# Lending two one-bank product tiles as a third score slot in the w_out stages

## The chip, the cores and the metric

The kernel runs on one core of one Trainium2 chip. The metric is device time in microseconds (us), median over several executions. All runs quoted here are of the undisturbed (fast) state; the granted TensorE clock was 0.996 to 1.000 of full speed in all of them, 0.998 to 1.000 in the profiled ones. Ratios are computed from the mean time of one kernel's fast runs over the mean time of the fast runs of the kernel before in the same rounds, so they are not quite the ratio of the quoted medians.

## The reference, cut to what matters

```python
# q, k, v: (8, 12, 448, 64)
scores = matmul(q, k.transpose(0, 1, 3, 2)) / sqrt(64)
attn   = maximum(scores, 0) ** 2 / 448
x      = matmul(attn, v)            # heads joined: (3584, 768)
h      = x @ w_in                   # (768, 2048)
g      = maximum(h, 0) ** 2
out    = g @ w_out                  # (2048, 768)
```

## The kernel before

TensorE is kept busy with the two dense stages, "w_in" (x @ w_in) and "w_out" (g @ w_out), in turn for each pair of batches. The attention of later batches is slipped in between as **visits**. A visit computes the scores of up to two tiles (four 64x64 matmuls each) and, when a head unit's seven tiles are squared, one attention-times-v unit (28 matmuls of 64x64), which I call an "av".

Scores go to one of two slots of two PSUM banks each; ScalarE evicts a slot with one ACTIVATE, and VectorE squares the result.

```python
def score(t, times=1, third=False):
    ...
    ps = slot(FP32, third)                      # two slots, two banks each
    ... nc.tensor.matmul(ps[c, hh, 0:S], ...)
    at = at_p.tile([P, 2, S], FP16, ...)
    nc.scalar.activation(out=at, in_=ps[:, :, 0:S], func=AF.Relu, scale=SK)
```

In w_out a **group** makes two row blocks by a scheme of seven products of eight matmuls each, numbered here 0 to 6 as in the code. They accumulate in two one-bank tiles X and Y; groups take turns between two pairs of such tiles. Product 0 of the next group is placed before product 5 of this one. At the end of a stage a mere six small w_in matmuls stand there.

```python
products = (                # accumulator, fresh, left, right, what follows
    (X, True,  ..., b11, end1),     # 0: copy m1 on ScalarE
    (Y, True,  ..., b21, end2),     # 1: output add on VectorE
    (X, False, ss[2], t2, end6),    # 2: copy u2 on ScalarE, then sum s3 on VectorE
    (Y, True,  ss[1], t1, end5),    # 3: sum s4 on VectorE
    (X, False, ss[3], t3, end7),    # 4: needs s3; copy u3 on ScalarE
    (X, False, ..., nt4, end4),     # 5: writes X again
    (Y, False, ss[4], b22, end3))   # 6: output add on VectorE
```

VectorE's order is planned on the host. The squares of a visit wait in a queue `due`; before a sum, those that the plan calls nearly ready are issued:

```python
def sums(i, rows, to):
    ...
    while due and due[0][0] <= max(at_ve[0], at_pe[0]) + 0.3:
        put(due)                    # a square
    now_ve(0.6)
    op(to[i], x, y)                 # the sum s1, s2, s3 or s4
...
def visit(tiles):                   # cut
    at_pe[0] += 0.19 + 0.19 * len(tiles)
    for i, t in enumerate(tiles):
        square(ats[t], 0.6 + 0.85 * i)
```

Of the kernel before, what the change touches and what calls it, by code (L numbers as in the profile page):

```python
# [12 lines left out]
FP32 = mybir.dt.float32  # L13
AF = mybir.ActivationFunctionType
# [4 lines left out]
def kernel(  # L19
# [9 lines left out]
    nc = tc.nc  # L29

    B, H, S, D = q.shape
    NT, DM = out.shape
# [11 lines left out]
    J = 7  # L44
    PW = S // J
    NU = 3
    NUN = B * NU
# [7 lines left out]
    SK = 256.0  # L55
    CX = 1.0 / 896.0
# [137 lines left out]
    def slot(dtype, third=False):  # L194
        return (third_p if third else s_p).tile(
            [P, 2, 2048 // mybir.dt.size(dtype)], dtype, name="slot", tag="slot")
# [54 lines left out]
    now = [0]  # L251
    avt = [None]

    def score(t, times=1, third=False):
        n, j = divmod(t, J)
        qT, kT = qkt[n]
        ps = slot(FP32, third)
        for hh in list(range(2)) * times:
            r = slice(64 * hh, 64 * hh + 64)
            for hp in range(2):  # L260
                c = slice(64 * hp, 64 * hp + 64)
                nc.tensor.matmul(  # L262
                    ps[c, hh, 0:S], lhsT=kT[r, j, c], rhs=qT[r, :, c],
                    start=True, stop=True)
        at = at_p.tile([P, 2, S], FP16, name="at", tag="at")
        nc.scalar.activation(out=at, in_=ps[:, :, 0:S], func=AF.Relu, scale=SK)  # L266
        ats[t] = at
        seen[t] = now[0]

# [28 lines left out]

    unit = [NU]

    def av_unit():

        n = unit[0]
        if n == NUN or seen.get(n * J + J - 1, 10 ** 6) >= now[0]:
            return
        unit[0] += 1
        flush(rest=False)
        at_pe[0] += 1.33
        b, u = divmod(n, NU)
        vt = vts[n]  # L310
        ps = slot(FP32)
        for j in range(J):
            at = ats.pop(n * J + j)
            for hp in range(2):
                r = slice(64 * hp, 64 * hp + 64)
                for hh in range(2):
                    nc.tensor.matmul(  # L317
                        ps[64 * hh:64 * hh + 64, hp, 0:S],
                        lhsT=vt[r, hh, j * D:(j + 1) * D], rhs=at[r, hh, :],
                        start=(j == 0), stop=(j == J - 1))  # L320
        if u == 0:
            xts[b] = x_p.tile([P, NM, S], FP16, name="xt", tag="xt")
        nc.scalar.activation(
            out=xts[b][:, 2 * u:2 * u + 2, :], in_=ps[:, :, 0:S],
            func=AF.Copy, scale=CX)

    def prefetch(m):
        if m >= NUN:
            return
        dma_transpose(m)  # L330
        if m > NPE:
            load_v(m)
        if m + 2 < NUN:
            load_qk(m + 2)
# [10 lines left out]
    def flush(rest=True):  # L345
        for d in (due, due_g) if rest else (due,):
            while d:
                put(d)

    def put(d):  # L350
        ready, cost, fn, _ = d.popleft()
        at_ve[0] = max(at_ve[0], at_pe[0], ready) + cost
        fn()

    def fill(until):
        for d in (due, due_g):
            while d and max(at_ve[0], at_pe[0], d[0][0]) + d[0][1] <= until:
                put(d)
# [8 lines left out]
    def square(at, lag=0.0):  # L367
        due.append((at_pe[0] + lag, 0.54,
                    lambda: nc.vector.tensor_mul(at, at, at), 0))  # L369

    def visit(tiles):
        now[0] += 1
        for t in tiles:
            if t % J == 0 and t >= NPE * J:
                prefetch(t // J + 2)
        for t in tiles[:1]:
            score(t)
        av_unit()
        for t in tiles[1:]:
            score(t)  # L380
        at_pe[0] += 0.19 + 0.19 * len(tiles)
        for i, t in enumerate(tiles):
            square(ats[t], 0.6 + 0.85 * i)
# [5 lines left out]
    def mm_tile(i=None, dtype=FP32):  # L389
        if i is None:  # L390
            mm_no[0] += 1
            i = mm_no[0] % len(big)
        return big[i].tile(
            [P, 2048 // mybir.dt.size(dtype)], dtype, name="mm", tag="mm")
# [45 lines left out]
    def sums_x(b, i):  # L440
        xt = xts[b]
        lo, hi = slice(0, NH), slice(NH, NM)
        b11, b12, b21, b22 = (xt[:, lo, 0:Q], xt[:, lo, Q:S], xt[:, hi, 0:Q],
                              xt[:, hi, Q:S])
        now_ve(0.42)
        if i != 2:
            t = late["xs"].tile([P, NH, Q], FP16, name=f"x{i}", tag=f"x{i}")
            xsum[b, i] = t
        if i == 0:
            nc.vector.tensor_sub(t, b12, b11)  # L450
        elif i == 1:
            nc.vector.tensor_sub(t, b22, xsum[b, 0])
        elif i == 2:
            nc.vector.tensor_sub(b12, b22, b12)
        else:
            nc.vector.tensor_sub(t, b21, xsum[b, 1])
# [139 lines left out]
    def o_groups(groups, then):  # L596
# [5 lines left out]
        def group(n, rows, last):  # L602
# [7 lines left out]
            def needs(k):  # L610

                return max(2 * p + (tb > 2) for p, tb in groups[k]
                           if (p, tb) not in saved)

            def ahead(i, k=n):
                if k < len(groups) and i not in sets[k]:
                    flush_g(needs(k))
                    sums(i, groups[k], sets[k])
# [95 lines left out]
            def step(k, f):  # L714
                acc, fresh, left, right, end = products[k]
                if last and k == 5:
                    acc, fresh = Z, True

                def run():
                    if f == 0 and fresh and k != 3:  # L720
                        acc[:] = [mm_tile((n + (k == 5)) % 2)]
                    if f == 0 and k == 0:
                        ahead(1)
                        ahead(2)
                    nc.tensor.matmul(  # L725
                        acc[0][:, 0:HALF], lhsT=left()[:, f], rhs=right[:, f],
                        start=(fresh and f == 0),
                        stop=(f == KH - 1), skip_group_check=not fresh)
                    if f == KH - 1:
                        end()  # L730
                        if k < 4 and n + 1 < len(groups):
                            some = sum(d[3] <= needs(n + 1) for d in due_g)
                            for _ in range(-(-some // (4 - k))):
                                put(due_g)
                        fill(at_pe[0] + AFTER[k])
                return run

            ls = [[(0.1625, step(k, f), ((2 if k == 5 else True) if f == 0 else False))
                   for f in range(KH)] for k in range(7)]
            if last:  # L740
                ls[6] = [(0.0825, step3(z, f), False) for z in range(2) for f in range(KH)]
# [34 lines left out]
    NB0 = NU * J  # L776
    ps = slot(FP32, True)
# [3 lines left out]
    def s(t, times=2):  # L781
        score(t, times, third=t in THIRD)
# [81 lines left out]
    def some(part):  # L864
# [11 lines left out]
        name="mmb", bufs=2, space=PSUM, side="right", reuse_waits="tile")))  # L876
    some(f0[4:6])
    visit([NB0, NB0 + 1])

    T_G = NM * 0.1892  # L880
# [5 lines left out]
    events = []  # L886
    seq = [[2, 3], 4, [4, 5], [6, 7], [8, 9], 5, [10, 11], [12, 13], [14, 15],
           [16, 17], [18, 19], [20], []]
    for i, ts in enumerate(seq):
        at = (2.5 + i) * T_G  # L890
        if isinstance(ts, int):
            events.append((at, lambda n=ts: pe_transpose(n)))
        else:
            events.append((at, lambda ts=ts: visit([NB0 + t for t in ts])))
# [14 lines left out]
    for m in (6, 7):  # L909
        events.append((T_H + (1 + 3 * (m - 6)) * T_G, lambda m=m: prefetch(m)))  # L910
    at0 = T_H + 8 * T_G
    for pr in range(1, B // 2):
        t0 = 2 * NB0 * pr
        end = begin[pr] + T_S - 6.5
        gap = (end - at0) / 21
        for i in range(21):
            ts = [t0 + 2 * i, t0 + 2 * i + 1]
            events.append((at0 + i * gap, lambda ts=ts: visit(ts), True))
        at0 = end
        for i in range(4):  # L920
            events.append((begin[pr] - 6 + i, lambda b=2 * pr, i=i: sums_x(b, i)))
    events.append((at0 + 0.3, lambda: visit([]), True))

    def pre(pr, i):
        def run():
# [29 lines left out]
                steps += periods[b, i0]  # L955
        steps += outs[pr][0]

    clock, last = 0.0, 0.0
    ev = deque(sorted(events, key=lambda e: e[0]))
    for cost, fn, edge in steps:  # L960
        fired = 0
        while ev and edge and ev[0][0] <= clock + (1.6 if edge == 2 and not fired else 1e-3):
            if len(ev[0]) == 3:
                if clock < last + 1.5:
                    break
                last = clock
            ev.popleft()[1]()
            fired += 1
        if fn is not None:
            at_pe[0] += cost  # L970
            fn()
        clock += cost
# [31 lines left out]
```

## Time and profile before

| | before |
|---|---|
| median of the first 3 runs (370.80 us with the fourth, run beside the changed kernel) | 370.99 us |
| profiled span | 368.9 us |
| TensorE busy | 359.6 us, 97% |
| VectorE, ScalarE busy | 265.4 us (72%), 247.5 us (67%) |
| visits from 60 us on | 64 |

In a row of the chain of waits the share is that of the span for which the line held up the end. In a timeline row the columns are the start and the length in us, engine, source line, operation, operands, how often, and in brackets the idle time before it with what ended it. Visits are counted as unbroken runs of 64x64 weight loads (PEld) between loads of 128x128.

### The profile page before, as it was taken

What the parts mean: (1) busy time and instruction counts of PE and PEld (TensorE: products, weight loads), DVE (VectorE), ACT (ScalarE), POOL (GpSimd) and SP (SyncE); (2) the same over time, 40 slices, a digit from 0 to 9 for tenths busy, and PEclk for the clock granted to TensorE, in tenths of its full rate; (3) what the DMA queues carried; (4) which work ended last, traced back from release to release, by engine and by line L of the source; (5) the groups of instructions that cost most, each with busy time, mean ns of one, the idle gap of its engine ahead of it and who ended that gap; (6) DMA issues with size and microseconds to landing.
All of it is one profiled execution on the core that took longest, in us unless ns stands there. A gap on an engine that the chain in (4) does not pass through costs nothing.

```text
span 368.9 us, 8720 instructions
## 1 busy us (share of the span) xinstructions
PE 359.6 (97%) x3588; PEld 230.3 (62%) x3588; DVE 265.4 (72%) x470; ACT 247.5 (67%) x371; POOL 107.1 (29%) x128
## 2 busy tenths in 40 slices
PE   8899999999999999999999999999999999999994
PEld 3644445445555778875555588786555689976663
DVE  2997677997777787788585766989766686884442
ACT  3988894787676989876556588886765885532220
POOL 8545521846553155531225045140000000000001
PEclk9999999999999999999999999999999999999999
DMA  8999999999999999967699899692323300003333
GB/s 115 191 207 203 205 204 162 161 158 165 190 166 127 184 101 98 115 93 62 140 166 105 159 155 86 88 116 37 65 71 88 85 3 2 2 0 85 87 92 81
DMA packets 121159, 42.64 MB, mean 116 GB/s; under 512 B 100832, under 2 KB 117760, under 8 KB 121120
## 3 DMA queue, kind: packets, MB, share of 16 engines
q0 software_dynamic: 82912, 23.01, 62.3%
q1 hardware_dynamic: 38048, 18.98, 25.7%
q8 instruction: 28, 0.46, 0.5%
q10 hardware_dynamic: 160, 0.10, 0.1%
q14 instruction: 11, 0.09, 0.1%
HBM read 45.61 MB, written 11.01 MB: 153 GB/s over the span
## 4 chain that ended last, share of the span: by engine, by line
PE 90%; ACT 3%; DVE 3%; issue 2%; DMA 1%; POOL 0%; POOLq 0%; ACTq 0%
PE mm L725 34%; PE mm L538 27%; PE slot L262 10%; PE mm L409 9%; PE slot L317 7%; ACT at L266 3%; DMA k<-in_k_dram 1%; DVE at L297 1%; PE avt L280 1%; PE slot L238 1%; PE mm L238 0%; DVE at L369 0%; DVE xt L292 0%; ACT u L627 0%; DVE osb L632 0%
## 5 line engine op out<-in xcount | busy, mean ns | idle before, releaser
L266 ACT ACTIVATE at<-slot 128x896 f16<-128x896 f32 x168 | 145.8, 925 | 22.2 <-PE slot L262 22.2
L369 DVE TENSOR_TENSOR at<-at 128x896 f16<-128x896 f16 x147 | 87.1, 617 | 9.7 <-ACT at L266 9.6
L109 POOL DMA_DIRECT2D qs<-in_q_dram x36 | 35.3, 983 | 113.7 <-DMA qT<-qs 106.2
L725 PEld LDWEIGHTS <-s 128*128 128x128 f16 x440 | 41.5, 98 | 32.7 <-issue 3.6
L262 PE MATMUL slot<-qT,kT 64*64 64x448 f16 x744 | 56.8, 361 | 1.9 <-ACT at L266 1.4
L538 PEld LDWEIGHTS <-w 128*128 128x128 f16 x576 | 54.3, 98 | 5.1 <-issue 4.3
L538 PE MATMUL mm<-xt,w 128*128 128x224 f16 x432 | 48.9, 259 | 0.0
L725 PEld LDWEIGHTS <-g 128*128 128x128 f16 x336 | 31.7, 98 | 24.1 <-issue 4.7
L538 PEld LDWEIGHTS <-ws 128*128 128x128 f16 x432 | 40.3, 98 | 4.7 <-issue 4.7
L632 DVE SCALAR_TENSOR_TENSOR osb<-mm,u 128x384 f32<-128x384 f32 (+1 forms) x30 | 16.2, 542 | 36.4 <-ACT u L627 24.0
L725 PE MATMUL mm<-b,g 128*128 128x384 f16 x224 | 40.7, 326 | 0.0
L725 PE MATMUL mm<-b,s 128*128 128x384 f16 x216 | 39.6, 326 | 0.2 <-DVE s L594 0.2
L409 PE MATMUL mm<-xt,w 128*128 128x448 f16 x192 | 39.8, 354 | 0.0
L725 PE MATMUL mm<-t,s 128*128 128x384 f16 x224 | 39.3, 326 | 0.0
L109 POOL DMA_DIRECT2D ks<-in_k_dram x36 | 35.1, 976 | 9.4 <-DMA b<-in_moe_w_out_dram 5.8
L262 PEld LDWEIGHTS <-kT 64*64 64x64 f16 x744 | 19.0, 104 | 28.7 <-issue 23.3
L561 POOL DMA_DIRECT2D out_dram<-osb x2 | 1.1, 563 | 119.6 <-DVE osb L632 119.6
L627 ACT ACTIVATE u<-mm 128x384 f32<-128x384 f32 x28 | 13.8, 492 | 31.6 <-PE mm L725 27.1
L538 PE MATMUL mm<-x,ws 128*128 128x224 f16 x288 | 34.1, 259 | 0.0
L481 DVE CUSTOM_DVE_ANT_0 g<-mm,m 128x448 f16<-128x448 f32 x36 | 22.4, 622 | 15.1 <-PE mm L538 7.3
L317 PE MATMUL slot<-at,vt 64*64 64x448 f16 x588 | 31.9, 350 | 0.2 <-DVE at L369 0.2
L409 PEld LDWEIGHTS <-w 128*128 128x128 f16 x192 | 17.1, 98 | 19.2 <-issue 5.1
(76 smaller groups left out, 399.7 us busy)
## 6 DMA issues: line engine op xcount, KB each, us to landing
out_dram<-osb SPq DMA_DIRECT2D x52, 192.0 KB, 3.0
vt<-in_v_dram POOLq DMA_DIRECT2D x24, 224.0 KB, 6.2
qs<-in_q_dram POOLq DMA_DIRECT2D x36, 112.0 KB, 4.6
ks<-in_k_dram POOLq DMA_DIRECT2D x36, 112.0 KB, 5.0
w<-in_moe_w_in_dram POOLq DMA_DIRECT2D x8, 384.0 KB, 11.9
b<-in_moe_w_out_dram POOLq DMA_DIRECT2D x4, 768.0 KB, 17.1
q<-in_q_dram POOLq DMA_DIRECT2D x6, 224.0 KB, 7.9
k<-in_k_dram POOLq DMA_DIRECT2D x6, 224.0 KB, 8.3
```

Source lines behind the costliest of these rows:

```text
L109: nc.gpsimd.dma_start(out=t[:, :, hh, :], in_=heads(src, n)[:, hh].rearrange("p (j d) -> p j d", d=D))
L238: nc.tensor.transpose(pss[i][64 * hh:64 * hh + 64, i if n < 4 else 0, j * P:(j + 1) * P], src[:, hh, j * D:(j + 1) * D], ident)
L262: nc.tensor.matmul(ps[c, hh, 0:S], lhsT=kT[r, j, c], rhs=qT[r, :, c], start=True, stop=True)
L266: nc.scalar.activation(out=at, in_=ps[:, :, 0:S], func=AF.Relu, scale=SK)
L317: nc.tensor.matmul(ps[64 * hh:64 * hh + 64, hp, 0:S], lhsT=vt[r, hh, j * D:(j + 1) * D], rhs=at[r, hh, :], start=(j == 0), stop=(j == J - 1))
L369: lambda: nc.vector.tensor_mul(at, at, at), 0))
L409: nc.tensor.matmul(cell[0][:, 0:S], lhsT=w1[f // 4][:, m, (f % 4) * P:(f % 4 + 1) * P], rhs=xts[b][:, m, :], start=(m == 0), stop=(m == NM ...
L481: nc.vector._custom_dve(TENSOR_ADD_SAT, out=gs(s, hi, right), in0=acc(s, y), in1=keep[s, nm], s0=3.4e38, s1=0.0)
L538: nc.tensor.matmul(XY[s][y][:, r * Q:(r + 1) * Q], lhsT=left(k, i0 + 2 * s + r, m), rhs=right(k, m), start=(fresh and r == 0 and m == 0), ...
L627: nc.scalar.activation(out=t, in_=X[0][:, 0:HALF], func=AF.Copy, scale=CO)
L632: nc.vector.scalar_tensor_tensor(out=osb[row][:, c], in0=acc[0][:, 0:cc.stop - cc.start], scalar=CO, in1=keep[nm][:, cc], op0=ALU.mult, op ...
L725: nc.tensor.matmul(acc[0][:, 0:HALF], lhsT=left()[:, f], rhs=right[:, f], start=(fresh and f == 0), stop=(f == KH - 1), skip_group_check=n ...
```

## The change

The intent is fewer visits. Ahead of products 2 and 4 of a group the other pair of product tiles is free for a moment. It is lent to the visit as a third slot, so that three tiles fit in one visit; where the visit has an av, the av takes the lent pair. The placing loop no longer has a fixed list of two-tile visits; it follows a planned count of tiles. So the edit changes two things at once, the number of tiles in a visit and the places of the visits; run e5 below keeps the new places and goes back to two tiles.

```diff
-    def score(t, times=1, third=False):
+    def score(t, times=1, third=False, ps=None):
-        ps = slot(FP32, third)
+        spare = ps is not None
+        ps = slot(FP32, third) if ps is None else [mm_tile(ps), mm_tile(ps)]
 ...
+        if spare:
+            for hh in range(2):
+                nc.scalar.activation(
+                    out=at[:, hh], in_=ps[hh][:, 0:S], func=AF.Relu, scale=SK)
+        else:
+            nc.scalar.activation(out=at, in_=ps[:, :, 0:S], func=AF.Relu, scale=SK)
 ...   (av_unit: the same, with two evictions of one bank)
+            edges = {2: (n + 1) % 2, 4: (n + 1) % 2}
 ...
+            ahead = tile_no - planned(clock)
+            elif pair is not None and ahead <= 1.5 and clock > last + 1.25:
+                n = min(3, NT - tile_no)
+                visit(list(range(tile_no, tile_no + n)), pair)
 ...
+            elif ahead <= (1.5 if soon else 0.0) and clock > last + 1.5:
+                n = min(2, NT - tile_no)
+                visit(list(range(tile_no, tile_no + n)))
```

More of the change, by code (lines that the diff above doesn't have):

```diff
@@ L262, in score @@
                 nc.tensor.matmul(
-                    ps[c, hh, 0:S], lhsT=kT[r, j, c], rhs=qT[r, :, c],
+                    ps[hh][c, 0:S] if spare else ps[c, hh, 0:S],
+                    lhsT=kT[r, j, c], rhs=qT[r, :, c],
                     start=True, stop=True)
         at = at_p.tile([P, 2, S], FP16, name="at", tag="at")
-        nc.scalar.activation(out=at, in_=ps[:, :, 0:S], func=AF.Relu, scale=SK)
+        if spare:
[4 more added lines that the diff above has]
+            nc.scalar.activation(out=at, in_=ps[:, :, 0:S], func=AF.Relu, scale=SK)
         ats[t] = at
@@ L299, with av_due, av_unit @@
     unit = [NU]
-    def av_unit():
+    def av_due():
         n = unit[0]
-        if n == NUN or seen.get(n * J + J - 1, 10 ** 6) >= now[0]:
+        return n < NUN and seen.get(n * J + J - 1, 10 ** 6) < now[0]
+    def av_unit(ps=None):
+        if not av_due():
             return
+        n = unit[0]
         unit[0] += 1
@@ L310, in av_unit @@
         vt = vts[n]
-        ps = slot(FP32)
+        spare = ps is not None
+        ps = [mm_tile(ps), mm_tile(ps)] if spare else slot(FP32)
         for j in range(J):
@@ L317, in av_unit @@
                     nc.tensor.matmul(
-                        ps[64 * hh:64 * hh + 64, hp, 0:S],
+                        ps[hp][64 * hh:64 * hh + 64, 0:S] if spare
+                        else ps[64 * hh:64 * hh + 64, hp, 0:S],
                         lhsT=vt[r, hh, j * D:(j + 1) * D], rhs=at[r, hh, :],
@@ L322, in av_unit @@
             xts[b] = x_p.tile([P, NM, S], FP16, name="xt", tag="xt")
+        if spare:
+            for hp in range(2):
+                nc.scalar.activation(
+                    out=xts[b][:, 2 * u + hp], in_=ps[hp][:, 0:S],
+                    func=AF.Copy, scale=CX)
+            return
         nc.scalar.activation(
@@ L369, in square, with visit @@
                     lambda: nc.vector.tensor_mul(at, at, at), 0))
-    def visit(tiles):
+    def visit(tiles, spare=None):
         now[0] += 1
@@ L376, in visit @@
         for t in tiles[:1]:
-            score(t)
-        av_unit()
+            score(t, ps=None if av_due() else spare)
+        av_unit(spare)
         for t in tiles[1:]:
@@ L736, in step @@
                 return run
-            ls = [[(0.1625, step(k, f), ((2 if k == 5 else True) if f == 0 else False))
+            edges = {2: (n + 1) % 2, 4: (n + 1) % 2}
+            ls = [[(0.1625, step(k, f),
+                    ((edges.get(k), k == 5) if f == 0 else False))
                    for f in range(KH)] for k in range(7)]
@@ L911 @@
     at0 = T_H + 8 * T_G
+    plan: list = []
     for pr in range(1, B // 2):
@@ L914 @@
         end = begin[pr] + T_S - 6.5
-        gap = (end - at0) / 21
-        for i in range(21):
-            ts = [t0 + 2 * i, t0 + 2 * i + 1]
-            events.append((at0 + i * gap, lambda ts=ts: visit(ts), True))
+        plan.append((at0, end, t0))
         at0 = end
@@ L921 @@
             events.append((begin[pr] - 6 + i, lambda b=2 * pr, i=i: sums_x(b, i)))
-    events.append((at0 + 0.3, lambda: visit([]), True))
     def pre(pr, i):
@@ L956, with planned @@
         steps += outs[pr][0]
-    clock, last = 0.0, 0.0
+    def planned(t):
+        n = 0.0
+        for a, e, t0 in plan:
+            if t >= a:
+                n = t0 + min(1.0, (t - a) / (e - a)) * 2 * NB0
+        return n
+    clock, last, tile_no = 0.0, 0.0, 2 * NB0
+    NT = NUN * J
     ev = deque(sorted(events, key=lambda e: e[0]))
     for cost, fn, edge in steps:
-        fired = 0
-        while ev and edge and ev[0][0] <= clock + (1.6 if edge == 2 and not fired else 1e-3):
-            if len(ev[0]) == 3:
-                if clock < last + 1.5:
-                    break
-                last = clock
-            ev.popleft()[1]()
-            fired += 1
+        while ev and edge and ev[0][0] <= clock + 1e-3:
+            ev.popleft()[1]()
+        if edge and clock >= plan[0][0]:
+            pair, soon = edge if edge is not True else (None, False)
+            ahead = tile_no - planned(clock)
+            if tile_no == NT:
+                if unit[0] < NUN and clock > last + 1.5:
+                    visit([])
+                    last = clock
+            elif pair is not None and ahead <= 1.5 and clock > last + 1.25:
+                n = min(3, NT - tile_no)
+                visit(list(range(tile_no, tile_no + n)), pair)
+                tile_no += n
+                last = clock
+            elif ahead <= (1.5 if soon else 0.0) and clock > last + 1.5:
+                n = min(2, NT - tile_no)
+                visit(list(range(tile_no, tile_no + n)))
+                tile_no += n
+                last = clock
         if fn is not None:
```

## The prediction

> **What bounds the kernel now.** I read the page first: the line of busy engines, the clock row, the chain that ended last. These are whole lines of it.
>
> ```profile
> PE 359.6 (97%) x3588; PEld 230.3 (62%) x3588; DVE 265.4 (72%) x470; ACT 247.5 (67%) x371; POOL 107.1 (29%) x128
> ...
> PEclk9999999999999999999999999999999999999999
> ...
> PE 90%; ACT 3%; DVE 3%; issue 2%; DMA 1%; POOL 0%; POOLq 0%; ACTq 0%
> PE mm L725 34%; PE mm L538 27%; PE slot L262 10%; PE mm L409 9%; PE slot L317 7%; ACT at L266 3%; DMA k<-in_k_dram 1%; DVE at L297 1%; PE avt L280 1%; PE slot L238 1%; PE mm L238 0%; DVE at L369 0%; DVE xt L292 0%; ACT u L627 0%; DVE osb L632 0%
> ```
>
> TensorE is the bound: nine tenths of the chain, at full clock. L725 is the w_out product, L262 the score of a tile, L317 the attention-times-v unit ("av" below). ScalarE and VectorE have a quarter to a third free, so they matter only where TensorE waits for one of their instructions.
>
> Second, the list of waits, for what TensorE (its weight loads) waits for:
>
> ```profile
> PEld L262 <- issue: 23.3, 80, 0.6
> ...
> PEld L725 <- issue: 8.3, 26, 0.4
> ...
> PEld L725 <- DVE s L594: 2.0, 5, 0.6
> ```
>
> Nothing but "issue" is large, and it comes once on entering a visit and once on leaving it. Waits for data are small: five for VectorE sums, 2.0 us in all.
>
> Third, the timeline of weight loads in the first w_out stage prices a visit:
>
> ```profile
> 80.24 2.39 PEld L725 LDWEIGHTS <-g 128*128 128x128 f16 x16 [0.20 <-issue]
> 82.95 0.14 PEld L262 LDWEIGHTS <-kT 64*64 64x64 f16 x8 [0.32 <-issue]
> 83.45 2.39 PEld L725 LDWEIGHTS <-s 128*128 128x128 f16 x16 [0.36 <-issue]
> 86.16 0.14 PEld L262 LDWEIGHTS <-kT 64*64 64x64 f16 x8 [0.32 <-issue]
> 86.66 1.09 PEld L725 LDWEIGHTS <-s 128*128 128x128 f16 x8 [0.36 <-DVE s L594]
> ```
>
> From 80.24 to 83.45 is 3.21 us for two products and a visit of two tiles. Sixteen 384-column matmuls stream in 16 x 0.1625 = 2.60 us (0.1625 is the code's own cost, and products without a visit between them start 1.30 to 1.31 us apart in the same timeline). So a two-tile visit costs 0.61 us. A tile is four 64x64 matmuls side by side over 448 columns, 448/2.4 GHz = 0.187 us, two make 0.375: **0.235 us is the fixed price of a visit**, and a third tile costs only 0.187.
>
> **What the Trainium skill says.** "TensorEngine Tiling (Array Packing)", section Key Properties: changing the tiling mode drains TensorE. The trace agrees: 64x64 visits between 128x128 products pay 0.235 us whatever their length. "TensorE: Matmul & The Clock Gate", in the section on the array being 16 small ones: ScalarE and VectorE are strict FIFO. That matters below, and the trace agrees (the copy at 287.15, further down). "ScalarE: Activation LUTs", section What ACT_TABLE_LOAD costs: an ACTIVATE with immediate operands takes 186 ns + 0.833 ns per column and neighbours overlap by about 93 ns. The trace has 925 ns for 896 columns and about 0.55 us for 448, with starts 0.81 and 0.44 us apart: two halves cost 0.88 in place of 0.81. "PSUM — Partial Sum Buffer", Terms: a bank may not be touched by two engines at once. So a lent product tile must first have been evicted; no run here shows a collision.
>
> **The change, part by part.** Removed: I stepped the placing loop's clock arithmetic for both versions. For before it gives 76 visits from the first pair on, at the places the chain of waits shows (18, 24, 18 small matmuls between visits in the second w_in stage). For after it gives 67. By w_out stage 11, 11, 10 become 10, 9, 7; the two w_in stages after the first and second w_out stage go from 13 and 11 to 11 and 10. The number of tiles and av units is the same. Nine visits x 0.235 = **-2.1 us**, all on the path.
>
> Added: 18 visits of three tiles, six in each of three w_out stages. In each a score or an av goes to two one-bank tiles and is evicted by two ACTIVATEs. That is 18 x 0.07 = 1.3 us on ScalarE, off the path.
>
> Moved: bursts get longer, and two chains behind a burst have TensorE waiting at their end. The end of the third w_out stage of before shows both, with two tiles. First TensorE, then ScalarE, then VectorE:
>
> ```profile
> 285.07 0.57 PE L262 MATMUL slot<-qT,kT 64*64 64x448 f16 x8
> 285.58 1.47 PE L725 MATMUL mm<-b,s 128*128 128x384 f16 x8
> 286.89 0.74 PE L538 MATMUL mm<-xt,w 128*128 128x224 f16 x6
> 287.69 1.46 PE L725 MATMUL mm<-nt,g 128*128 128x384 f16 x8
> ```
> ```profile
> 285.51 1.73 ACT L266 ACTIVATE at<-slot 128x896 f16<-128x896 f32 x2 [1.09 <-PE slot L262]
> 287.15 0.49 ACT L627 ACTIVATE u<-mm 128x384 f32<-128x384 f32 x1
> ```
> ```profile
> 204.02 0.62 DVE L369 TENSOR_TENSOR at<-at 128x896 f16<-128x896 f16 x1 [0.18 <-ACT at L266]
> 204.56 0.68 DVE L594 TENSOR_TENSOR s<-g 128x1024 f16<-128x1024 f16 x1
> ```
>
> *Chain A, the copy u3.* Product 5 overwrites the bank of product 4, so it waits for the copy of that bank, which stands on ScalarE behind the visit's evictions. Before: visit at 285.07, copy ends 287.64, product 5 starts 287.69; unhindered it would have started at 286.89 + 6 x 0.0958 = 287.46, a wait of 0.23. After, from the visit's start: evictions begin at +0.44, then 0.88 (halves) + 0.81 + 0.82 gives the copy at +2.95, its end at +3.44, product 5 at +3.48. Unhindered, at a stage end, product 5 could start at 0.50 + 0.19 + 1.30 + 0.57 = +2.56: **0.92 us lost**. With an av in the visit both sides move (xt evictions from +1.77, copy ends +4.77, unhindered +3.89): 0.92 again. The placing loop puts a three-tile visit ahead of product 4 and none ahead of product 5 at all three stage ends: 2.77 us. Inside a stage a whole product of the next group (1.30, not 0.57) lies between: 0.19 us, and nothing where a visit is placed before product 5.
>
> *Chain B, the sum s3.* Product 4 needs a VectorE sum that is issued when product 2 ends. The code first issues every square whose planned time is at most 0.3 us away, and advances its own clock by 0.54 for each: third square planned at 2.30 after the visit, clock then 2.38, so the third square also goes ahead of the sum. Its tile is evicted at +3.05; square to +3.68, sum to about +4.29, product 4 at +4.35 from the visit before product 2. Unhindered it would start at 0.69 + 2.60 = +3.29 if no visit stands before product 4 (groups 0 and 2 of the second stage: **1.06 lost each**), and at +4.08 with a three-tile visit there (0.27 lost), and late enough with an av in that visit (nothing). The last fence is before's own case, with two tiles: a visit at 201.82, the square at 204.02, the sum, and product 4 at 205.30 in place of 204.93.
>
> Sum of waits after, by stage. First: 0.27 in group 0 and 0.92 at the end, 1.2. Second: 1.06 + 0.27 + 1.06 + 0.92 = 3.3. Third: 0.19 + 0.27 + 0.92 = 1.4. **+5.9 us**. Where a group meets both chains I took the longer. Removed with the old placing are the waits at the three stage ends of before: 0.47 (an av visit of 2.30 us at 113.75 in place of 1.83), 0.37 and 0.23, together **-1.1**. Net: -2.1 - 1.1 + 5.9 = +2.7, so 371.0 + 2.7 = 373.7 us.
>
> **The rivals.** *Pure saving*: the waits do not arise, because the planner's order or a following visit hides them; then 371.0 - 2.1 - 1.1 = 367.8, or about 369 with a third of the waits. For it: TensorE waits for data hardly at all in before, and both other engines have idle time. Against: that idle time is not behind a burst, and before already shows both chains biting with two tiles. *The lent tiles themselves block*: the pair before product 2 is the other group's Y bank, read by VectorE after product 6, only one product earlier. If VectorE is late by 0.5 us there, up to nine visits lose 0.5 each, for some 376 to 378. Against: in the timeline of before, product 6 ends and that read starts at about 93.85 and 94.01, 106.7 and 106.87, 188.2 and 188.39, 200.45 and 200.65, and only once half a microsecond apart (176.0 and 176.52); and after product 4 the lent halves are evicted by +1.0 to +2.3 while the next writer comes at +2.0 to +3.3. *Ends that cancel*: the two chains overlap more than I take, so half of 5.9 remains; 370.8.
>
> **Range and chances.** I lean a little from 373.7 to the cancelling rival, since the waits are each differences of two estimated times: **373.0 us**. The range 370.0 to 375.4 runs from half of the waits to all of them plus some blocking. Two per cent is 7.4 us: the most that the saving can give is 3.2 and the waits would have to more than double, so within 2% has 0.97, slower 0.02, faster 0.01.
>
> **What would show it.** Right: the number of weight-load entries into visits falls by nine, a three-tile visit is about 0.19 us longer than a two-tile one; TensorE waits of about 0.9 us ahead of product 5 at three stage ends with a copy u just ended on ScalarE; waits of about 1 us for the sums s in two groups of the second w_out stage; "PEld L725 <- DVE s" rising from 2.0 to some 4 us. Wrong: no such waits and a time near 368 (pure saving), or L262 and L317 waiting for the output adds or copies (the lent tiles block). A slower clock or later transfers would be something that I did not see at all.

## The result

The changed kernel took **373.86 us** (373.29 to 374.24, 4 runs) against 370.8 us, a ratio of 1.0081 with a 95% interval of 1.0063 to 1.0098. It is slower, by 0.8%: clear of the noise, less than the 2% that the prediction was asked about, and inside its range of 370.0 to 375.4.

The profile's page of the changed kernel, busy times and then the chain by engine:

```profile
PE 358.6 (96%) x3588; PEld 231.7 (62%) x3588; DVE 265.8 (71%) x470; ACT 249.2 (67%) x389; POOL 107.2 (29%) x128
...
PE 85%; ACT 6%; DVE 3%; issue 2%; DMA 2%; POOLq 0%; POOL 0%; ACTq 0%
```

TensorE does the same work (3588 matmuls), ScalarE has 18 instructions and 1.7 us more. The chain now passes through ScalarE for 6% of the span, where it was 3%: TensorE has begun to wait for it.

The list of waits of the changed kernel (L746 is the w_out product, L263 the score, L615 the sums, L648 the copies m1, u2 and u3; the last three numbers are us in total, how often, and the longest):

```profile
PEld L263 <- issue: 20.5, 69, 0.6
...
PEld L746 <- DVE s L615: 6.2, 9, 1.3
...
PE mm L746 <- DVE s L615: 2.6, 7, 0.9
...
PE mm L746 <- ACT u L648: 1.6, 3, 0.7
```

Entries into visits fell by eleven, from 80 to 69, in this list: nine visits, one entry that stands under another label, and one pause inside a visit that is gone. From 60 us on there are 55 visits in place of 64, nine fewer. The idle time of the weight loads before a sum grew from 2.0 to 6.2 us, with a longest of 1.3. Not all of that is waiting: the usual pause on leaving a visit, 0.36 us with two tiles, is in it, and four of the five entries of the kernel before are no longer than that. The matmuls themselves (PE) waited for a sum once in the kernel before, for 0.2 us, and seven times here, for 2.6 us. There are also three waits of products for a copy u.

The **long wait for a sum**, in the first group of the second w_out stage. The timeline of weight loads, then that of VectorE:

```profile
167.36 0.41 PEld L263 LDWEIGHTS <-kT 64*64 64x64 f16 x12 [0.32 <-issue]
168.05 2.39 PEld L746 LDWEIGHTS <-s 128*128 128x128 f16 x16 [0.28 <-issue]
171.69 1.09 PEld L746 LDWEIGHTS <-s 128*128 128x128 f16 x8 [1.25 <-DVE s L615]
```
```profile
170.41 0.62 DVE L388 TENSOR_TENSOR at<-at 128x896 f16<-128x896 f16 x1 [0.18 <-ACT at L273]
170.96 0.68 DVE L615 TENSOR_TENSOR s<-g 128x1024 f16<-128x1024 f16 x1
```

The visit loads twelve weights, three tiles. Products 2 and 3 follow at once. Product 4 starts 4.33 us after the visit (171.69 - 167.36). Its sum was ready at 171.64 and stood behind the square that waited until 170.41 for the third eviction.

The **stage end**, here the third w_out stage. Weight loads, then ScalarE:

```profile
287.71 0.33 PEld L263 LDWEIGHTS <-kT 64*64 64x64 f16 x12 [0.32 <-issue]
288.64 1.09 PEld L746 LDWEIGHTS <-s 128*128 128x128 f16 x8 [0.60 <-DVE s L615]
289.79 0.64 PEld L559 LDWEIGHTS <-w 128*128 128x128 f16 x6
290.44 0.10 PEld L746 LDWEIGHTS <-g 128*128 128x128 f16 x1
291.16 1.07 PEld L746 LDWEIGHTS <-g 128*128 128x128 f16 x7 [0.63 <-issue]
```
```profile
288.13 0.98 ACT L270 ACTIVATE at<-mm 128x448 f16<-128x448 f32 x2 [0.42 <-PE mm L263]
288.99 1.73 ACT L273 ACTIVATE at<-slot 128x896 f16<-128x896 f32 x2
290.58 0.53 ACT L648 ACTIVATE u<-mm 128x384 f32<-128x384 f32 x1
```

ScalarE works without a pause from 288.13: two halves, two whole tiles, the copy u3, which ends at 291.11. Product 5 goes on at 291.16, 3.45 us after the visit. The weight load at 290.44 had gone ahead, but its matmul could not start; the pause is labelled "issue" although ScalarE was what ended it. The matmuls' own row above, `PE mm L746 <- ACT u L648`, names it.

**A balance of all visits.** To see where the difference lies as a whole I took, for each visit, the time from its first matmul to that of the next visit, less the streaming time of the matmuls in between (0.1625 us for a w_out matmul, 0.0958 for a small w_in one, 0.187 for a tile, 1.31 for an av). The figure for a tile agrees with the timelines: from a visit's first weight load to the next product's it is 0.50 us with two tiles (82.95 to 83.45 in the prediction) and 0.69 with three (167.36 to 168.05). What is over has a median of 0.24 us in both kernels: the fixed price of a visit. I call the rest waits. The last visit has no successor and is left out.

| from the profiled runs, us | visits | over in all | visits x 0.24 | waits |
|---|---|---|---|---|
| before | 63 | 16.56 | 15.12 | 1.44 |
| after | 54 | 19.23 | 12.96 | 6.27 |

The price of visits fell by 2.16 and the waits rose by 4.83, +2.67 in all, of the 2.9 us by which the spans differ.

### The profile page after: what moved, and what is told of

It reads as the page before. It is cut to its first block, busy times and chain, and to the rows that moved or that the text cites. A ratio compares the mean times of both kernels' runs of the same rounds, so it can differ in the third digit from the quotient of the medians.

```text
span 371.8 us, 8752 instructions
## 1 busy us (share of the span) xinstructions
PE 358.6 (96%) x3588; PEld 231.7 (62%) x3588; DVE 265.8 (71%) x470; ACT 249.2 (67%) x389; POOL 107.2 (29%) x128
## 4 chain that ended last, share of the span: by engine, by line
PE 85%; ACT 6%; DVE 3%; issue 2%; DMA 2%; POOLq 0%; POOL 0%; ACTq 0%
PE mm L746 31%; PE mm L559 26%; PE mm L430 9%; PE slot L263 8%; PE slot L329 5%; ACT at L273 4%; PE mm L329 2%; DMA q<-in_q_dram 1%; DVE at L304 1%; DMA out_dram<-osb 1%; ACT at L270 1%; DVE s L615 1%; PE mm L263 1%; PE avt L287 1%; PE slot L238 1%
## 5 line engine op out<-in xcount | busy, mean ns | idle before, releaser
L273 ACT ACTIVATE at<-slot 128x896 f16<-128x896 f32 x156 | 135.2, 928 | 10.1 <-PE slot L263 10.1
L746 PEld LDWEIGHTS <-s 128*128 128x128 f16 x440 | 41.4, 98 | 35.7 <-DVE s L615 6.2
L263 PE MATMUL slot<-qT,kT 64*64 64x448 f16 x696 | 52.5, 358 | 1.9 <-ACT at L273 1.4
L746 PEld LDWEIGHTS <-g 128*128 128x128 f16 x336 | 32.2, 98 | 24.7 <-issue 4.7
L746 PE MATMUL mm<-b,s 128*128 128x384 f16 x216 | 39.6, 327 | 2.6 <-DVE s L615 2.6
L746 PE MATMUL mm<-b,g 128*128 128x384 f16 x224 | 40.9, 326 | 0.0
L746 PE MATMUL mm<-t,s 128*128 128x384 f16 x224 | 38.8, 327 | 0.0
L263 PEld LDWEIGHTS <-kT 64*64 64x64 f16 x744 | 19.7, 105 | 27.5 <-issue 20.5
L648 ACT ACTIVATE u<-mm 128x384 f32<-128x384 f32 x28 | 14.4, 513 | 25.8 <-PE mm L746 23.8
L508 DVE TENSOR_TENSOR g<-g 128x896 f16<-128x896 f16 x48 | 28.8, 617 | 0.4 <-ACT g L511 0.4
```

The source lines that it names most:

```text
L263: nc.tensor.matmul(ps[hh][c, 0:S] if spare else ps[c, hh, 0:S], lhsT=kT[r, j, c], rhs=qT[r, :, c], start=True, stop=True)
L508: lambda: nc.vector.tensor_mul(g, g, g), b))
L648: nc.scalar.activation(out=t, in_=X[0][:, 0:HALF], func=AF.Copy, scale=CO)
L746: nc.tensor.matmul(acc[0][:, 0:HALF], lhsT=left()[:, f], rhs=right[:, f], start=(fresh and f == 0), stop=(f == KH - 1), skip_group_check=n ...
```

## The experiments

My theory had a saving (nine visits, 0.235 us each) and two losses: chain A, the copy u3 behind three evictions, and chain B, the sum s3 behind the third square. The rivals are that the lent tiles or their split evictions cost the time, that one chain alone does, and that fewer visits are worth nothing. Five rounds were run for each kernel; all outputs were right.

**e1: sum first.** Chain B alone is taken away.

```diff
-        while due and due[0][0] <= max(at_ve[0], at_pe[0]) + 0.3:
+        while i != 3 and due and due[0][0] <= max(at_ve[0], at_pe[0]) + 0.3:
```

> The changed kernel with one condition added: the third sum of a group is issued on VectorE before any pending squares. Theory (chain B, the sum behind the third square, costs 1.04 us in two groups of the second w_out stage and 0.24 us in three others): the waits 'PEld L746 <- DVE s' shrink from 6.2 us to under 3; the two long ones can give back only 0.85 each because the copy u2, behind the same three evictions, then binds at 3.48 us after the visit in place of 4.33; in all about 2.0 us, so some 371.8 us. Rival 1 (the lent tiles and their split evictions cost the time): no change, 373.9. Rival 2 (only the stage ends, chain A, matter): no change, 373.9.

Measured: 371.45 us, ratio 1.0023 (1.0010 to 1.0035), so 2.4 us came back by the medians (2.2 by the ratios) where 2.0 were expected. In the whole list of waits of this run no weight load waits for a sum any more. The two long visits now have 0.38 over in place of 1.28 and 1.27, that is 0.14 above the fixed price; in the first of them it is the copy u2 that now ends the wait (it ends at 170.77, product 4 starts at 170.82). Chain B is real, and both rivals of that text fall. One row of the list grew, from 1.6 to 2.1 us:

```profile
PE mm L746 <- ACT u L648: 2.1, 3, 0.7
```

At the ends of the first and third stage both chains fall in one group. There the wait for the sum went, but the visits still have 1.11 over, because the wait for the copy took its place.

**e9: only the third square moved.**

```diff
-            square(ats[t], 0.6 + 0.85 * i)
+            square(ats[t], (0.6, 1.45, 2.9)[i])
```

> The changed kernel with one number altered: the planned time of the third square of a visit is 2.9 us after the visit in place of 2.3, so that just this one square is issued after the third sum, the first two still before it. Theory (it is the third square, not the squares as such, that puts the sum late): product 4 comes some 3.54 us after the visit in place of 4.33 in the two long cases and without a wait in the short ones; 1.9 us come back, nearly what the sum-first edit gave (2.4): about 371.9 us. Rival (any square ahead of the sum costs, so two of three still cost most of it): 373.2 or more.

Measured: 371.89 us, ratio 1.0022 (1.0009 to 1.0034), nearly the same as e1. The weight loads of the same place as above in this run:

```profile
167.21 0.41 PEld L263 LDWEIGHTS <-kT 64*64 64x64 f16 x12 [0.32 <-issue]
167.90 2.39 PEld L746 LDWEIGHTS <-s 128*128 128x128 f16 x16 [0.28 <-issue]
170.73 1.09 PEld L746 LDWEIGHTS <-s 128*128 128x128 f16 x8 [0.44 <-DVE s L615]
```

Product 4 comes 3.52 us after the visit, against 4.33, with two squares still ahead of the sum. It is the third square that matters, and its eviction, which is the last of three.

**e2: u3 of a stage's last group on VectorE.** Chain A alone, at the stage ends.

```diff
+                if vector:
+                    nc.vector.tensor_scalar(out=t, in0=X[0][:, 0:HALF],
+                        scalar1=CO, scalar2=None, op0=ALU.mult)
...
-                copy("u3")
+                copy("u3", n + 1 == len(groups))
```

> The changed kernel with the copy u3 of the last group of a stage made by VectorE (a tensor_scalar) in place of ScalarE, so that it does not stand behind the evictions of the three-tile visit. Theory (chain A costs 0.9 us at three stage ends): in the second stage nearly all 0.87 come back; in the first and third VectorE is busy with sums until just before, so only some 0.2 each; about 1.3 us, 372.6 us. Rival 1 (lent tiles) and a rival in which only chain B counts: 373.9.

Measured: 372.59 us, ratio 1.0048 (1.0036 to 1.0061), 1.3 us back, as worked out. The visit at the end of the second stage has 0.49 over in place of 1.12; at the other two 0.91 in place of 1.11, because VectorE was at its sums until just before.

**e3: both edits.**

> Both edits together. Theory: with the sums out of the way earlier, the VectorE copy is on time at all three stage ends, so 2.0 + some 2.3 us come back: about 369.5 us, faster than the kernel before (370.8), because the saving of nine visits at 0.235 us is then no longer eaten. Rival 1 (lent tiles): 373.9 still. Rival 3 (the waits hide one another, so that taking both away gives less than the sum of the two single edits, 3.3): above 370.6.

Measured: **369.34 us**, ratio 0.9967 (0.9953 to 0.9980): faster than the kernel before, by 0.3%. By the medians the two single edits gave 2.4 and 1.3 us, both together 4.5 (by the ratios 2.2, 1.2 and 4.2); with the sums earlier the copy on VectorE is on time. The end of the third stage in this run, weight loads:

```profile
284.25 0.33 PEld L263 LDWEIGHTS <-kT 64*64 64x64 f16 x12 [0.32 <-issue]
284.94 1.09 PEld L753 LDWEIGHTS <-s 128*128 128x128 f16 x8 [0.36 <-DVE x L471]
...
287.07 1.07 PEld L753 LDWEIGHTS <-g 128*128 128x128 f16 x7 [0.23 <-issue]
```

Product 5 goes on 2.82 us after the visit, against 3.45.

**e10: sum first, and no third tile ahead of product 4 in a stage's last group.** This takes chain A away by the placing, with no work moved.

```diff
-            edges = {2: (n + 1) % 2, 4: (n + 1) % 2}
+            edges = {2: (n + 1) % 2, 4: (n + 1) % 2 if n + 1 < len(groups) else None}
```

> Sum first, and no lent pair ahead of product 4 in the last group of a stage, so no three-tile visit there: by the placing loop's arithmetic 69 visits in place of 67. Theory (chain A at the stage ends is what is left, 2.7 us): it goes, two visits at 0.235 us come back, and three more groups have the copy u2 0.2 us late; so 371.45 - 2.7 + 0.5 + 0.6 = 369.9 us, without any work moved to VectorE. Rival (the vector copy helped for another reason, such as a lighter ScalarE): 371.4 or more.

Measured: 370.55 us, ratio 0.9989 (0.9976 to 1.0001). That is below e1, so chain A is confirmed without a lighter ScalarE, but 0.6 above my figure. The balance below shows why: two visits more than e1, and the waits fell by 1.5, not by 2.1 (2.7 less 0.6). Moving the visits made new waits inside av visits (0.60 over at 177.7 us, 0.86 at 109.2 where e1 has 0.72), which I had not counted. This was read from the trace, not tried.

**e7: sum first, u3 on VectorE in every group.** The edit is that of e2 with `copy("u3", True)`.

> Sum first, and the copy u3 made by VectorE in every group, not only the last of a stage. Theory: the waits of 0.21 us ahead of product 5 inside the stages, three of them, go too: some 0.5 us below the kernel with both edits, 368.8 us. Rival: the extra 0.5 us of VectorE work per group comes before squares that TensorE waits for, and it is no better, 369.3 or more.

Measured: **368.91 us**, ratio 0.9947 (0.9935 to 0.9960), the fastest of the versions run: 0.5% under the kernel before, 1.3% under the changed kernel. The step from e3 is not sure: the two intervals overlap a little.

**e5: lent tiles, but two tiles a visit.**

```diff
-                n = min(3, NT - tile_no)
+                n = min(2, NT - tile_no)
```

> The changed kernel with two tiles in place of three in the visits that have a lent pair, everything else kept: by the placing loop's arithmetic 76 visits again, 20 of them with a lent pair. Theory (the bursts of three cost, not the lending): the long waits go, the saving of nine visits too; between 370.5 and 372, near the kernel before. Rival 1 (lent tiles block, or split evictions cost): it stays at 373 or more, with L263 or L329 on TensorE waiting for output adds or copies.

Measured: 370.33 us, ratio 0.9994 (0.9981 to 1.0006): no difference from the kernel before is shown. Twenty visits used lent tiles and split evictions, at the new places, and together these cost nothing that can be seen. The burst of three is what costs, not the lending and not the new placing.

**e4: both edits in the kernel before.**

> The kernel before with the two edits (sum first, the last u3 of a stage on VectorE) and its own placing of two-tile visits. Theory: it had about 1.0 us of such waits at the stage ends, of which the edits can take some 0.4 to 0.6: 370.2 to 370.4 us, still above the changed kernel with both edits (369.3), since it makes nine visits more. Rival (the edits are worth 4.5 us to any placing, the visits nothing): 366.3.

Measured: 370.80 us, ratio 0.9996 (0.9983 to 1.0010), no difference shown; the small gain that I expected would be at the edge of what these rounds can tell. The edits are not simply worth 4.5 us anywhere: they are worth it where visits have three tiles.

**e11: e7 with two tiles a visit.** The nine visits come back, the two edits stay.

> The kernel with sum first and u3 on VectorE in every group (368.9 us, 0.9947 of the kernel before), with one number altered: two tiles in place of three in the visits with a lent pair, so that the nine visits saved are made after all (64 in place of 55 from 60 us on). Theory (a visit has a fixed price of 0.235 us on TensorE): 2.1 us dearer, less at most 0.5 us for waits behind the bursts of three that are left there: 370.5 to 371.0 us. Rival (fewer visits are worth nothing, the two edits gave the whole gain): 368.9 again, or less.

Measured: 369.80 us, ratio 0.9974 (0.9961 to 0.9988). Fewer visits are worth something, 1.0 us by the ratios ((0.9974 - 0.9947) x 370.8), but I had expected 1.6 to 2.1. The balance tells what I missed: e7 still has 1.7 us of waits where I had reckoned with 0.5 above this kernel's, and e11 has 0.4. The visits differ by 0.84 us over in all, 2.16 saved less 1.32 of waits. And e11, which saves no visit, is itself 0.3% faster than the kernel before: about half of what e7 gained comes from somewhere other than fewer visits, from the two edits with the new placing.

**The balance for all runs**, made as above. The fifth column sets the whole against before; the last is the measured median less the median of the kernel before of the same rounds.

| run | visits | over in all | waits | against before | measured |
|---|---|---|---|---|---|
| before | 63 | 16.56 | 1.44 | | |
| after | 54 | 19.23 | 6.27 | +2.7 | +3.1 |
| e1 sum first | 54 | 17.17 | 4.21 | +0.6 | +0.7 |
| e9 third square | 54 | 17.30 | 4.34 | +0.7 | +0.9 |
| e2 u3 on VectorE | 54 | 18.19 | 5.23 | +1.6 | +1.9 |
| e3 both | 54 | 15.21 | 2.25 | -1.4 | -1.4 |
| e7 both, all u3 | 54 | 14.65 | 1.69 | -1.9 | -2.1 |
| e10 no third at end | 56 | 16.19 | 2.75 | -0.4 | -0.5 |
| e5 lent, two tiles | 63 | 15.84 | 0.72 | -0.7 | -0.4 |
| e4 before, both edits | 63 | 16.24 | 1.12 | -0.3 | -0.2 |
| e11 two tiles, edits | 63 | 15.49 | 0.37 | -1.1 | -1.0 |

Price of visits plus waits follows the measured time within 0.4 us in every run. That shows where the time lies, in the stretches around visits and not in the products or before and after them. It can't show why, since "waits" is whatever is left over; the causes rest on the timelines and on the single edits.

## Why the prediction was right, point by point

- **The saving**: nine visits at 0.235 us, -2.1. Right: 64 to 55 visits, a median price of 0.24, 2.16 us in the balance. The price did not grow with the third tile: in e7 the twelve three-tile visits without an av have a median of 0.24 too.
- **Chain A**: 0.92 us at each of three stage ends. Right: product 5 came 3.45 us after the visit in the first and third stage and 4.78 in the second, where I had 3.48 and 4.81; against the unhindered times of the prediction that is 0.89 us each. e2 and e10 show that the copy is the cause.
- **Chain B**: 1.06 us in groups 0 and 2 of the second stage, 0.27 in shorter cases. Right: product 4 came 4.33 us after the visit in both long cases (1.04), and 0.24 late in the short ones. e1 and e9 show that the third square is the cause.
- **The sum of the waits**: +5.9 - 1.1 = +4.8. The balance has +4.83, but the parts are not all mine, so that so close an agreement is luck. One wait that I counted as removed, at the end of the first stage, came back elsewhere: in group 2 of that stage the av visit at 109.20 us waits about 0.5 us for squares of the visit just before. In e3, e7 and e10 it is still there. The waits that I had listed came to about 5.6 in place of 5.9, which made up for most of it.
- **Where I chose wrongly**: the parts gave 373.7 us, and I moved to 373.0 towards the rival of ends that cancel. The measured 373.86 gives no ground for that. The chains do hide one another where they meet in one group (e1, at two stage ends), but the prediction had counted only the longer one there; nothing more was hidden, and both edits together give more than the sum of the single ones.
- **What I misread**: the 2.0 us of `PEld L725 <- DVE s` is mostly the usual pause after a visit, so my sign "some 4 us" was badly set; the row came to 6.2. The VectorE fence under "Moved" is from the end of the second stage, not of the third, as its time of 204.02 shows. And I started from 371.0 where the kernel before ran at 370.8: the change was +3.0 us by the ratio, and my parts gave +2.7.
- **The rivals**: the pure saving is excluded by the result. That the lent tiles block: in the changed kernel's whole list, no visit's weight load or matmul waits for an output add or a copy u, and e5 shows no cost.

What stays open: the remaining 1.7 us of waits in e7 were not each tried (the largest, about 0.5 us, is in the av visit at 108.96 us); and in e4 and e5 the rounds cannot tell an effect of 0.1% from none.

## What to carry to other kernels

When visits to a side task are merged, the fixed price saved is easy to count, but the bursts grow: follow the last eviction of the longer burst to every instruction that stands behind it on an in-order engine, and ask when the bottleneck engine needs that one. Here a saving of 2.2 us was paid for with 4.8 us of waits. With two small reorderings (the urgent sum ahead of the squares, the urgent copy on the other engine) the kernel ended 2.1 us under the kernel before, and 1.0 us of that is what the merging itself was worth (e7 against e11). A planner with hand-set readiness times has to be set anew when the burst changes.

## What the Trainium skill lacked or had wrong

- "TensorEngine Tiling (Array Packing)", section Key Properties, says that a change of the tiling mode drains TensorE, but gives no figure: here entering and leaving a 64x64 visit between 128x128 products costs 0.24 us together (median of 63 visits in the kernel before; 0.25 for those with an av). That this is the drain, and not some other part of the change, no run here separates.
- "ScalarE: Activation LUTs", section What ACT_TABLE_LOAD costs: its 186 ns + 0.833 ns per column fits (0.925 us for 896 columns, about 0.54 for 448). Its overlap of about 93 ns between neighbours is a little more here: in the kernel before, neighbouring evictions of 896 columns overlap by 0.115 us (median of 77 pairs).
- No page that I read says how a wait of a matmul whose weights were loaded ahead appears in a profile: the 0.63 us ahead of the rest of product 5's weight loads at 291.16 us is labelled "issue", though the end of a ScalarE copy at 291.11 us released the matmul.
